# An output projection in halves, full-array masks and sums, and a new order of values and tails in a recurrent attention layer

## Chip, cores, metric

The kernel runs on one core of one Trainium2 chip. The metric is the time of one execution on the device in microseconds (us).

## The reference, cut to what matters

Two kinds of layer alternate, A B A B, over 2048 tokens of 640 features. Layer B is the one that changes. It is a recurrence of 64 steps; each takes 32 tokens and the 8 memory rows that the step before it produced.

```python
for s in range(n_seg):
    h = jnp.concatenate([mem, xs], axis=1)            # 8 + 32 rows
    q, k, v = (einsum('btd,dhe->bhte', h, W) for W in (Wq, Wk, Wv))   # 32 heads of 128
    p = softmax(where(mask, q @ k.T * scale, -1e9))
    o = einsum('bhte,hed->btd', p @ v, Wo)
    mem = o[:, :M, :]                                  # goes into the next step
    outs.append(o[:, M:, :])
```

## The kernel before

All of a step's matrices are thin (32 rows), so nearly all matmuls run as four column tiles of 32 columns side by side. A step does, for its two halves of 16 heads: Q and K (b_Qa, b_Ka, b_Qb, b_Kb), each turned by a 32x32 transpose on DVE; mask and scores into b_SP; exp on ACT; sums over the keys by matmuls with ones; Ln and Exp of the sums on ACT, a product on DVE; V (b_V), the values (b_OTL, four row tiles), their copy to SBUF (b_OTsb), the O projection (b_OPS). The last 8 of each step's 32 tokens go apart, four steps at a time: their Q, K and V for the next four steps ("tails", b_tail) and their O projection for the last four ("deferred O", b_OPSd) serve as filling between. Of every four steps one carries the deferred O, one a layer norm with five full-array transposes (b_lntps).

```python
# O projection: per head four column tiles of 160 columns, 128 matmuls a step
for q in range(4):
    nc.tensor.matmul(self.ps[32*q:32*q+32, :], lhsT=self.src_fn(h), rhs=W.wo[:, h, 160*q:160*q+160],
                     start=(self.p == 0 and e == 0), stop=..., tile_position=(0, 32*q), ...)
...
# order of the second half of a step
vpass(0); scores(1); vpass(1); sums(1); values(0); normalise(1)
take("act", 0, 0); take("act", 0, 1)          # copies of the values to SBUF
fill(1.0)
op.run(4); values(1); take("dve", 1, 0); take("act", 1, 1); op.run(4); op.run(8)
...                                           # transpose of O's memory rows, into the next step's h
fill(9)
```

PSUM has three banks for Q, K, V, scores and tails (b_ps), one for O, two pairs for the values.

## Time and profile before

| | before |
|---|---|
| time | 2634.66 us, median of 3 (2625.54 to 2636.77) |
| TensorE busy | 87% |
| steps of layer B | 126 from start to start, mean 14.76 us: 1860 us |
| instruction packets of 16,384 bytes | 512 |

In the lines of the profile PE is TensorE's matmuls and PEld its weight loads, DVE the vector engine, ACT the scalar engine, POOL GpSimd, SPq the queue that starts transfers; L87 is a line of the kernel (here that of a helper), "<-" leads from what is written to what is read, and "issue" is a wait for nothing that the profile shows. A matmul and its weight load are called a pair.

The prediction below shows the lines of the page, of the waits and of the timeline that carry its argument. One more stretch is from the timeline of TensorE alone: start and length in us, the instruction, output and inputs, shapes, count. A length holds the latency of the last matmul, so what a stage costs is read from its start to the next stage's start.

```profile
426.79 1.28 PE L87 MATMUL b_Kb<-b_wk,b_hT 128*32 128x512 bf16 x20
427.87 0.28 PE L87 MATMUL b_SP<-b_PT,b_blk 128*32 128x160 bf16 x6
...
427.98 1.27 PE L87 MATMUL b_V<-b_wv,b_hT 128*32 128x512 bf16 x19
429.04 0.28 PE L87 MATMUL b_SP<-b_mask,c_identb 128*32 128x160 bf16 x4
429.21 0.37 PE L87 MATMUL b_SP<-b_QT,b_KT 128*32 128x40 bf16 x32
429.43 1.27 PE L87 MATMUL b_V<-b_wv,b_hT 128*32 128x512 bf16 x20
```

Kb takes 1.08 us, sums 0.11, V0 1.06, the second mask 0.17 (0.07 of it work, the rest a wait for K), the scores 0.22: 2.64 us from Kb to V1.

### The profile page before, as it was taken

To read this page: it belongs to the slowest core of one execution; us is meant where nothing else is said; L and a number is where in the kernel's file an instruction comes from. 1 tells how busy PE (TensorE), PEld (TensorE's weight loads), DVE (VectorE), ACT (ScalarE), POOL (GpSimd) and SP (SyncE) were. 2 spreads that over 40 slices of the span, in tenths; PEclk is the share of its full clock that TensorE was granted. 3 is DMA by queue.
4 is the path that set the end of the run, shared out by engine and by line. 5 is a ranking of instruction groups with operands and counts; after the bars stand their busy time and mean duration, and the time that the engine had idled before them with its cause. 6 is when DMAs were issued, how large, how long until landed. Compare 5 with 4: busy or idle time off the path is not lost.

```text
span 2645.6 us, 144539 instructions
## 1 busy us (share of the span) xinstructions
PE 2301.3 (87%) x65166; PEld 1440.4 (54%) x65228; DVE 1600.3 (60%) x3743; ACT 882.3 (33%) x2067; POOL 992.5 (38%) x2333
## 2 busy tenths in 40 slices
PE   6878879999989889888769778799999998989996
PEld 3444446556656556555534444466666665665654
DVE  5666646666656556665556666466666666666654
ACT  5665712222222222222146557122222222222221
POOL 2333434333433334333223334334434333334332
PEclk9888989999999999999978889899999999999999
DMA  6662341111100111100033233400100000101000
GB/s 180 153 162 88 96 132 23 24 22 22 22 22 22 23 23 23 24 19 19 21 97 100 85 101 106 136 19 20 22 20 19 20 20 20 21 19 22 17 17 16
DMA packets 118388, 133.20 MB, mean 50 GB/s; under 512 B 31856, under 2 KB 103552, under 8 KB 115840
## 3 DMA queue, kind: packets, MB, share of 16 engines
q1 hardware_dynamic: 116160, 122.21, 17.6%
q8 instruction: 512, 8.39, 1.4%
q10 hardware_dynamic: 1600, 1.66, 0.2%
q14 instruction: 116, 0.95, 0.1%
HBM read 89.17 MB, written 26.21 MB: 44 GB/s over the span
## 4 chain that ended last, share of the span: by engine, by line
PE 70%; DVE 8%; issue 8%; ACT 3%; POOL 2%; DMA 1%; SPq 0%; DVEq 0%; POOLq 0%; ACTq 0%
PE b_OPS L87 12%; PE b_V L87 11%; PE b_tail L87 8%; PE b_Qa L87 6%; PE b_Ka L87 5%; PE b_Kb L87 5%; PE b_SP L87 4%; PE b_Qb L87 4%; PE b_OTL L87 3%; PE b_OPSd L87 3%; PE a_PP L87 3%; ACT a_PT L87 2%; DVE b_TQ L87 2%; PE a_S L87 2%; DVE a_qk L87 1%
## 5 line engine op out<-in xcount | busy, mean ns | idle before, releaser
L87 PEld LDWEIGHTS <-b_hT 128*32 128x32 bf16 x15520 | 466.3, 96 | 319.4 <-issue 63.7
L87 PE MATMUL b_OPS<-b_wo,b_OTsb 128*32 128x160 bf16 x16384 | 365.8, 234 | 58.9 <-issue 50.9
L87 ACT ACTIVATE b_PT<-b_SP 128x224 bf16<-128x224 f32 x256 | 91.5, 358 | 947.3 <-PE b_SP L87 931.1
L87 PEld LDWEIGHTS <-b_OTsb 128*32 128x32 bf16 x16384 | 289.2, 97 | 120.3 <-issue 68.3
L87 ACT ACTIVATE a_PT<-a_S 128x768 bf16<-128x768 f32 (+1 forms) x384 | 325.5, 891 | 83.5 <-PE a_S L87 76.6
L87 PE MATMUL b_V<-b_wv,b_hT 128*32 128x512 bf16 x5120 | 330.0, 380 | 10.7 <-DVE b_TQ L87 7.9
L87 POOL CAST b_QT<-b_TQ 128x384 bf16<-128x384 f32 x254 | 140.8, 554 | 292.7 <-DVE b_TQ L87 292.5
L87 DVE TENSOR_TENSOR b_PT<-b_PT,b_R 128x160 bf16<-128x160 bf16 (+1 forms) x512 | 215.5, 461 | 45.2 <-ACT b_R L87 44.9
L87 POOL TENSOR_TENSOR b_Rtot<-b_Rtot,b_R 128x160 bf16<-128x160 bf16 x256 | 142.8, 558 | 265.3 <-ACT b_R L87 247.8
L87 DVE STREAM_TRANSPOSE b_TQ<-b_Qa 128x512 f32<-128x512 f32 x128 | 91.8, 717 | 206.8 <-PE b_Qa L87 204.8
L87 POOL CAST b_KT<-b_TQ 128x384 bf16<-128x384 f32 x254 | 142.5, 561 | 181.2 <-DVE b_TQ L87 181.1
L87 DVE CAST b_Vsb<-b_V 128x512 bf16<-128x512 f32 x256 | 175.2, 684 | 34.2 <-PE b_V L87 30.5
L87 ACT CAST b_OTsb<-b_OTL 128x320 bf16<-128x320 f32 x384 | 148.7, 421 | 136.1 <-PE b_OTL L87 136.1
L87 PE MATMUL b_Qa<-b_wq,b_hT 128*32 128x512 bf16 x2560 | 172.5, 381 | 21.0 <-DVE b_hT L87 10.0
L87 POOL TENSOR_SCALAR_AFFINE_SELECT a_PT<-a_PT 128x256 bf16<-128x256 bf16 x256 | 109.2, 431 | 214.1 <-ACT a_PT L87 201.1
L87 PE MATMUL b_Ka<-b_wk,b_hT 128*32 128x512 bf16 x2560 | 170.6, 383 | 0.1
L87 PE MATMUL b_Qb<-b_wq,b_hT 128*32 128x512 bf16 x2560 | 168.1, 380 | 0.0
L87 PE MATMUL b_Kb<-b_wk,b_hT 128*32 128x512 bf16 x2560 | 163.1, 379 | 3.1 <-DVE b_xnbd L87 2.2
L87 PE MATMUL a_PP<-a_xnT,a_wt 128*128 128x512 bf16 x505 | 148.9, 409 | 9.6 <-issue 5.4
L87 DVE STREAM_TRANSPOSE b_TM<-b_OPS 128x160 f32<-128x160 f32 x126 | 43.7, 347 | 187.2 <-PE b_OPS L87 187.0
L87 PE MATMUL a_S<-a_qk 32*128 32x512 bf16 (+3 forms) x1024 | 143.9, 323 | 7.1 <-ACT a_PT L87 5.8
L87 PEld LDWEIGHTS <-b_hx 128*32 128x32 bf16 x3840 | 101.2, 97 | 85.6 <-issue 25.1
(162 smaller groups left out, 3834.7 us busy)
## 6 DMA issues: line engine op xcount, KB each, us to landing
a_wt<-a_wpad SPq DMA_DIRECT2D x112, 160.0 KB
b_wo<-in_B_Wo_dram SPq DMA_DIRECT2D x8, 1280.0 KB
b_XO<-xres SPq DMA_DIRECT2D x512, 15.0 KB
b_Vt<-b_Vtb SPq DMA_DIRECT2D x512, 16.0 KB
a_wvo<-in_A_wo_dram SPq DMA_DIRECT2D x8, 800.0 KB
b_wq<-in_B_Wq_dram SPq DMA_DIRECT2D x20, 256.0 KB
b_wk<-in_B_Wk_dram SPq DMA_DIRECT2D x20, 256.0 KB
xres<-a_xo SPq DMA_DIRECT2D x16, 320.0 KB
```

The source lines that it names most:

```text
L87: r = f(*a, **k)
```

## The change

Its intent is fewer and larger TensorE instructions, and an order that hides the copies and the softmax of the second half.

```diff
 # O in halves: two heads at a time, two column tiles each, 320 columns; the two partial sums are added later
-  for q in range(4):
-      matmul(ps[32*q:32*q+32, :160], lhsT=src(h), rhs=W.wo[:, h, 160*q:160*q+160], tile_position=(0, 32*q))
+  for jj2 in range(2):
+      q = 2 * e + jj2
+      matmul(ps[32*q:32*q+32, :320], lhsT=src(h), rhs=W.wo[:, h, 320*jj2:320*jj2+320], tile_position=(0, 32*q))
...
-  nc.vector.tensor_tensor(out=XO[:], in0=ops[:], in1=XO[:], op=ALU.add)                     # 128 x 160
+  nc.vector.tensor_tensor(out=XO[0:64, :], in0=ops[0:64, :], in1=XO[0:64, :], op=ALU.add)   # 64 x 320, twice
+  nc.vector.tensor_tensor(out=XO[0:64, :], in0=ops[64:128, :], in1=XO[0:64, :], op=ALU.add)
...
 # mask: one full-array matmul; sums: block-diagonal ones, 4 full-array matmuls for 8 tiled ones
-  for j in range(4):
-      matmul(sp[32*j:32*j+32, :, 0:40], lhsT=C.identb[:, 32*j:32*j+32], rhs=mask4, tile_position=(0, 32*j))
+  matmul(sp[:, :, 0:40], lhsT=C.identb[:], rhs=mask4)
...
 # the softmax's reciprocals in the layout of the weights: one product for two
-  tensor_tensor(PT[:, b, :, 16:56] *= R);  tensor_tensor(PT[:, b, :, 0:16] *= R[:, :, 24:40])
+  tensor_tensor(PT[:, b] *= R)
...
 # order
-  vpass(1); sums(1); values(0); normalise(1); take(0, 0); take(0, 1); fill(1.0)
-  op.run(4); values(1); take(1, 0); take(1, 1); op.run(4); op.run(8)
+  V1.run(3); values(0); V1.run(2); sums(1); take(0, 0); take(0, 1); normalise(1)
+  op.run(4); op.run(4); fill(0.44); values(1); fill(0.66)
+  take(1, 0); take(1, 1); flush(); op.run(8)        # flush: turns of finished tails, deferred till here
...
-  late.append(store_deferred)      # residual of the deferred O: after Ka of the next step
+  store_deferred(T - 1, u)         # at once
```

The rows of Wq, Wk, Wv, of the layer norm's output and of the memory are permuted to fit the halves; the layer norm's statistics and its application are taken apart, and in one step of four the residual of O itself is stored at once too.

More of the change, by code (lines that the diff above doesn't have):

```diff
@@ L56, in build_consts, with layernorm_stats @@
     return C
-def layernorm_tile(nc, pool, C, xt, xn_out, name):
+def layernorm_stats(nc, pool, C, xt, name):
     stats = pool.tile([128, 2, nc.vector.BN_STATS_DIM], F32, name=f"{name}_st", tag="ln_st")
@@ L67, in layernorm_tile, with layernorm_apply @@
     nc.gpsimd.tensor_tensor(out=rstd[:], in0=rstd[:], in1=C.mhalf[:, 0:1], op=ALU.pow)
-    nc.vector.tensor_scalar(out=xn_out.rearrange("p (g q d) -> p q g d", q=4, d=32),
-                            in0=xt.rearrange("p (q g d) -> p q g d", q=4, d=32),
+    return mv, rstd
+def layernorm_apply(nc, xt, xn_out, mv, rstd):
+    nc.vector.tensor_scalar(out=xn_out.rearrange("p (g jj d) -> p jj g d", jj=2, d=32),
+                            in0=xt.rearrange("p (jj g d) -> p jj g d", jj=2, d=32),
                             scalar1=mv[:, 0:1], scalar2=rstd[:, 0:1], op0=ALU.subtract, op1=ALU.mult)
@@ L574, in load_B_weights @@
         setattr(W, nm, t)
-        sv = src.rearrange("(q g d) h e -> g q d (h e)", q=4, d=32)
+        sv = src.rearrange("(jj g d) h e -> g jj d (h e)", jj=2, d=32)
         for c in range(NCH):
@@ L578, in load @@
                 for q in range(4):
-                    nc.sync.dma_start(t[32 * q:32 * q + 32, c, :], sv[c, q])
+                    nc.sync.dma_start(t[32 * q:32 * q + 32, c, :], sv[2 * c + q // 2, q % 2])
             loads.append(load)
@@ L606, in pair_tile @@
             return pot.tile([128, 2, 512], F32, name=name, tag="ot")
-        ones = st.tile([128, 128], BF16, name="b_ones")
-        nc.vector.memset(ones[:], 1.0)
+        if general:
+            ones = st.tile([128, 128], BF16, name="b_ones")
+            nc.vector.memset(ones[:], 1.0)
         blk = st.tile([128, 2, 4, 32], BF16, name="b_blk")
@@ L615, in layer_B @@
         if not general:
-            Rtot = st.tile([128, 160], BF16, name="b_Rtot")
+            Rtot = st.tile([128, 4, 40], BF16, name="b_Rtot")
             nc.vector.memset(Rtot[:], 0.0)
-        XO = st.tile([128, 160], F32, name="b_XO")
+        XO = st.tile([64, 320], F32, name="b_XO")
         nc.vector.memset(XO[:], 0.0)
@@ L661, in ln_norm, with ln_apply @@
             xt = ln_x.pop(g)
-            xn = wk.tile([128, D], BF16, name="b_xn", tag="xn")
-            layernorm_tile(nc, sm, C, xt[:], xn[:], "b_ln")
-            ln_n[g] = xn
+            ln_n[g] = xt, layernorm_stats(nc, sm, C, xt[:], "b_ln")
+        def ln_apply(g):
+            xt, (mv, rstd) = ln_n[g]
+            xn = ln_n[g] = wk.tile([128, D], BF16, name="b_xn", tag="xn")
+            layernorm_apply(nc, xt[:], xn[:], mv, rstd)
         def ln_tr(g):
@@ L733, in tail_cols @@
             if T not in hx:
-                hx[T] = wk2.tile([128, NCH, 32], BF16, name="b_hx", tag="hx")
+                hx[T] = wk.tile([128, NCH, 32], BF16, name="b_hx", tag="hx")
                 v = xnT_g[T][:].rearrange("p c (i t) -> p c i t", t=32)[:, :, :, 24:32]
@@ L764, in run, with finish, flush @@
                     if not self.parts:
-                        if self.kind == "V":
-                            evac("act", Vtb[self.T][:, self.b, :], self.ps[:])
-                        else:
-                            d = QTt if self.kind == "Q" else KTt
-                            place("pool", turn(self.ps[:]), self.b, d[self.T], 0, 32, 0)
-                return k
+                        done.append(self.finish)
+                return k
+            def finish(self):
+                if self.kind == "V":
+                    evac("act", Vtb[self.T][:, self.b, :], self.ps[:])
+                else:
+                    d = QTt if self.kind == "Q" else KTt
+                    place("pool", turn(self.ps[:]), self.b, d[self.T], 0, 32, 0)
+        done = []
+        def flush():
+            while done:
+                done.pop(0)()
         def tails_to_seg(s):
@@ L788, in run @@
                 if self.ps is None:
-                    self.ps = self.pool.tile([128, 160], F32, name=self.name, tag=self.tag)
+                    self.ps = self.pool.tile([128, 320], F32, name=self.name, tag=self.tag)
                 while k > 0 and self.p < 16:
@@ L792, in run @@
                         h = self.horder[2 * self.p + e]
-                        for q in range(4):
-                            nc.tensor.matmul(self.ps[32 * q:32 * q + 32, :], lhsT=self.src_fn(h), rhs=W.wo[:, h, 160 * q:160 * q + 160],
-                                             start=(self.p == 0 and e == 0), stop=(self.p == 15 and e == 1),
-                                             tile_position=(0, 32 * q), skip_group_check=True)
+                        for jj2 in range(2):
+                            q = 2 * e + jj2
+                            nc.tensor.matmul(self.ps[32 * q:32 * q + 32, :], lhsT=self.src_fn(h), rhs=W.wo[:, h, 320 * jj2:320 * jj2 + 320],
+                                             start=(self.p == 0), stop=(self.p == 15), tile_position=(0, 32 * q), skip_group_check=True)
                     self.p += 1
@@ L801, in add_out @@
         def add_out(ops, XO, name):
+            nc.vector.tensor_tensor(out=XO[0:64, :], in0=ops[0:64, :], in1=XO[0:64, :], op=ALU.add)
             if out_bf16:
-                xnb = wk.tile([128, 160], BF16, name=name, tag=name)
-                nc.vector.tensor_tensor(out=xnb[:], in0=ops[:], in1=XO[:], op=ALU.add)
+                xnb = wk.tile([64, 320], BF16, name=name, tag=name)
+                nc.vector.tensor_tensor(out=xnb[0:64, :], in0=ops[64:128, :], in1=XO[0:64, :], op=ALU.add)
                 return xnb
-            nc.vector.tensor_tensor(out=XO[:], in0=ops[:], in1=XO[:], op=ALU.add)
+            nc.vector.tensor_tensor(out=XO[0:64, :], in0=ops[64:128, :], in1=XO[0:64, :], op=ALU.add)
             return XO
@@ L818, in layer_B @@
             nc_raw.sync.dma_start(W.wo[:, 8 * q:8 * q + 8, :], wo_src[:, 8 * q:8 * q + 8, :])
-        ln_norm(0); ln_tr(0)
+        ln_norm(0); ln_apply(0); ln_tr(0)
         alloc_h(0)
-        nc.vector.tensor_copy(m0[:, 1, :].rearrange("p (g q d) -> p q g d", q=4, d=32),
-                              m0[:, 0, :].rearrange("p (q g d) -> p q g d", q=4, d=32))
+        nc.vector.tensor_copy(m0[:, 1, :].rearrange("p (g jj d) -> p jj g d", jj=2, d=32),
+                              m0[:, 0, :].rearrange("p (jj g d) -> p jj g d", jj=2, d=32))
         mt = ps_tile([128, NCH, 8], BF16, "b_m0T")
@@ L830, in layer_B @@
                 TailUnit(0, kind, b).run(NCH)
+                flush()
         for Wt, dst in ((W.wq, QT), (W.wk, KT)):
@@ L836, in layer_B @@
         tails_to_seg(0)
-        ln_dma(1); ln_norm(1); ln_tr(1)
+        ln_dma(1); ln_norm(1); ln_apply(1); ln_tr(1)
         deferred = {}
         XOd = {}
-        def deferred_rows(x, T_, q):
-            v = x.rearrange("(t i k) d -> t i k d", i=4, k=32)
-            return v[T_, :, 24:32, 160 * q:160 * q + 160]
         def load_deferred(T_):
-            XOd[T_] = wk.tile([128, 160], F32, name="b_XOd", tag="XOd")
-            for q in range(4):
-                nc.sync.dma_start(XOd[T_][32 * q:32 * q + 32, :], deferred_rows(x_src, T_, q))
+            XOd[T_] = wk.tile([64, 320], F32, name="b_XOd", tag="XOd")
+            for jj2 in range(2):
+                for i in range(4):
+                    r = 32 * (4 * T_ + i) + 24
+                    nc.sync.dma_start(XOd[T_][32 * jj2 + 8 * i:32 * jj2 + 8 * i + 8, :], x_src[r:r + 8, 320 * jj2:320 * jj2 + 320])
         xn_pending = []
@@ L932, in scores @@
                 sp = t[:, 0:224].rearrange("p (r c) -> p r c", c=56)
-                for j in range(4):
-                    nc.tensor.matmul(sp[32 * j:32 * j + 32, :, 0:40], lhsT=C.identb[:, 32 * j:32 * j + 32],
-                                     rhs=mask[:].unsqueeze(1).to_broadcast([128, 4, 40]),
-                                     start=True, stop=False, tile_position=(0, 32 * j), skip_group_check=True)
+                nc.tensor.matmul(sp[:, :, 0:40], lhsT=C.identb[:], rhs=mask[:].unsqueeze(1).to_broadcast([128, 4, 40]),
+                                 start=True, stop=False, skip_group_check=True)
                 for r in range(4):
@@ L955, in sums @@
             def sums(b):
-                sm_ = SP[b][:, 256:416].rearrange("p (r c) -> p r c", c=40)
+                sm_ = SP[b][:, 256:480].rearrange("p (r c) -> p r c", c=56)
                 for k in range(2):
-                    for j in range(4):
-                        o = sm_[32 * j:32 * j + 32, :, 24 * k:40]
-                        nc.tensor.matmul(o, lhsT=blk[:, k, j, :], rhs=PT[:, b, :, 0:16] if k else PT[:, b, :, 16:56],
-                                         start=(k == 0), stop=(k == 1), tile_position=(0, 32 * j), skip_group_check=True)
@@ L964, in normalise @@
-            def normalise(b):
-                R = sm.tile([128, 160], F32, name="b_R", tag="R")
-                nc.scalar.activation(out=R[:], in_=SP[b][:, 256:416], func=ACT.Ln)
-                nc.scalar.activation(out=R[:], in_=R[:], func=ACT.Exp, scale=-1.0)
-                Rv = R[:].rearrange("p (r c) -> p r c", c=40)
-                nc.vector.tensor_tensor(out=PT[:, b, :, 16:56], in0=PT[:, b, :, 16:56], in1=Rv, op=ALU.mult)
-                nc.vector.tensor_tensor(out=PT[:, b, :, 0:16], in0=PT[:, b, :, 0:16], in1=Rv[:, :, 24:40], op=ALU.mult)
+                    lhsT = blk[:, k].rearrange("p j n -> p (j n)")
@@ new lines, in sums @@
+                    first, last_ = (k == 0), (k == 1)
+                    nc.tensor.matmul(sm_[:, :, 40 * k:56] if k else sm_[:, :, 16:56], lhsT=lhsT,
+                                     rhs=PT[:, b, :, 0:16] if k else PT[:, b, :, 16:56],
+                                     start=first, stop=last_, skip_group_check=True)
+                    nc.tensor.matmul(sm_[:, :, 0:16], lhsT=lhsT, rhs=PT[:, b, :, 0:16] if k else PT[:, b, :, 40:56],
+                                     start=False, stop=last_, skip_group_check=True)
@@ L972, in normalise @@
+            def normalise(b):
+                R = wk.tile([128, 4, 56], F32, name="b_R", tag="R")
+                flat = R[:].rearrange("p r c -> p (r c)")
+                nc.scalar.activation(out=flat, in_=SP[b][:, 256:480], func=ACT.Ln)
+                nc.scalar.activation(out=flat, in_=flat, func=ACT.Exp, scale=-1.0)
+                nc.vector.tensor_tensor(out=PT[:, b], in0=PT[:, b], in1=R[:], op=ALU.mult)
                 if not general:
-                    nc.gpsimd.tensor_tensor(out=Rtot[:], in0=Rtot[:], in1=R[:], op=ALU.add)
+                    nc.gpsimd.tensor_tensor(out=Rtot[:], in0=Rtot[:], in1=R[:, :, 16:56], op=ALU.add)
@@ L989, in take, with __init__, run @@
                 evac(eng, OTsb[:, h:h + 8, :].rearrange("p (j r) c -> p j (r c)", j=2), OTL[b, jp][:, :, 0:160])
-            def vpass(b):
-                V = ps_tile([128, 512], F32, "b_V")
-                thin_mm(V, vcols, W.wv, b, w_cols)
-                evac("dve", Vsb[:, b, :], V[:])
+            class VPass:
+                def __init__(self, b):
+                    self.b = b
+                    self.ps = ps_tile([128, 512], F32, "b_V")
+                    self.parts = thin_parts(self.ps, vcols, W.wv, b, w_cols)
+                def run(self, k=NCH):
+                    while k > 0 and self.parts:
+                        self.parts.pop(0)()
+                        k -= 1
+                    if not self.parts:
+                        evac("dve", Vsb[:, self.b, :], self.ps[:])
             qk(W.wq, "b_Qa", 0, QT)
@@ L999, in layer_B @@
                 late.pop(0)()
-            for q in range(4):
-                nc.sync.dma_start(XO[32 * q:32 * q + 24, :], x_src[32 * s:32 * s + 24, 160 * q:160 * q + 160])
+            for jj2 in range(2):
+                nc.sync.dma_start(XO[32 * jj2:32 * jj2 + 24, :], x_src[32 * s:32 * s + 24, 320 * jj2:320 * jj2 + 320])
             qk(W.wq, "b_Qb", 1, QT)
@@ L1014, in layer_B @@
                 row_max(1)
-            vpass(0)
+            VPass(0).run()
             scores(1)
-            vpass(1)
+            V1 = VPass(1)
+            V1.run(3)
+            values(0)
+            g_need = (s + 6) // 4 if s % 4 == 2 else NT
+            if g_need < NT:
+                ln_norm(g_need)
+            V1.run(2)
             sums(1)
-            values(0)
-            normalise(1)
             take("act", 0, 0)
             take("act", 0, 1)
+            normalise(1)
+            if g_need < NT:
+                ln_apply(g_need)
+                xn_pending.append(g_need)
             if i4 != 3:
                 tails_to_seg(s + 1)
-            fill(1.0)
             op = OPass(lambda h: OTsb[:, h, 0:32], HORDER, "b_OPS", po, "op")
             op.run(4)
+            op.run(4)
+            fill(0.44)
             values(1)
+            fill(0.66)
             take("dve", 1, 0)
             take("act", 1, 1)
-            op.run(4)
+            flush()
             op.run(8)
             ops = op.ps
-            g_need = (s + 6) // 4
-            if s % 4 == 2 and g_need < NT:
-                ln_norm(g_need)
-                xn_pending.append(g_need)
             if not general:
@@ L1046, in layer_B @@
             if not last:
-                TM = wk.tile([128, NCH, 32], F32, name="b_TM", tag="TM")
+                TM = wk.tile([128, 10, 32], F32, name="b_TM", tag="TM")
                 nc.vector.transpose(out=TM[:].rearrange("p g t -> p (g t)"), in_=ops[:])
-                nc.vector.tensor_copy(hT[s + 1][:, :, 24:32], TM[:, :, 24:32])
+                for hf in range(2):
+                    nc.vector.tensor_tensor(out=hT[s + 1][64 * hf:64 * hf + 64, :, 24:32], in0=TM[0:64, hf:10:2, 24:32],
+                                            in1=TM[64:128, hf:10:2, 24:32], op=ALU.add)
             fill(9)
+            flush()
             if not last and i4 == 3:
@@ L1056, in store @@
                 xo = add_out(ops, XO, "b_xnb")
-                for q in range(4):
-                    nc.sync.dma_start(x_dst[32 * s:32 * s + 24, 160 * q:160 * q + 160], xo[32 * q:32 * q + 24, :])
-            late.append(store)
+                for jj2 in range(2):
+                    nc.sync.dma_start(x_dst[32 * s:32 * s + 24, 320 * jj2:320 * jj2 + 320], xo[32 * jj2:32 * jj2 + 24, :])
+            if i4 == 1:
+                store()
+            else:
+                late.append(store)
             def store_deferred(T_, od):
@@ L1064, in store_deferred @@
                 xd = add_out(od.ps, XOd.pop(T_), "b_xnbd")
-                for q in range(4):
-                    nc.sync.dma_start(deferred_rows(x_dst, T_, q), xd[32 * q:32 * q + 32, :])
+                for i in range(4):
+                    for jj2 in range(2):
+                        r = 32 * (4 * T_ + i) + 24
+                        nc.sync.dma_start(x_dst[r:r + 8, 320 * jj2:320 * jj2 + 320], xd[32 * jj2 + 8 * i:32 * jj2 + 8 * i + 8, :])
             for u in units:
                 if isinstance(u, OPass):
-                    late.append(lambda u=u, T=T: store_deferred(T - 1, u))
+                    store_deferred(T - 1, u)
             if last:
@@ L1078, in layer_B @@
             rt = sm.tile([128, 1], F32, name="b_rt", tag="seen")
-            nc.vector.tensor_reduce(out=rt[:], in_=Rtot[:], axis=AX.X, op=ALU.add)
+            nc.vector.tensor_reduce(out=rt[:], in_=Rtot[:].rearrange("p r c -> p (r c)"), axis=AX.X, op=ALU.add)
             nc.vector.tensor_tensor(out=C.tot[:, 1, 0:1], in0=C.tot[:, 1, 0:1], in1=rt[:], op=ALU.add)
```

## The prediction

> **What bounds the kernel now.** The chip ran 2634.66 us (median of 3). I read the page first: which engine is busy, the chain that ended last, and the costliest groups.
>
> ```profile
> PE 2301.3 (87%) x65166; PEld 1440.4 (54%) x65228; DVE 1600.3 (60%) x3743; ACT 882.3 (33%) x2067; POOL 992.5 (38%) x2333
> ...
> q8 instruction: 512, 8.39, 1.4%
> ...
> PE 70%; DVE 8%; issue 8%; ACT 3%; POOL 2%; DMA 1%; SPq 0%; DVEq 0%; POOLq 0%; ACTq 0%
> ...
> L87 PE MATMUL b_OPS<-b_wo,b_OTsb 128*32 128x160 bf16 x16384 | 365.8, 234 | 58.9 <-issue 50.9
> ```
>
> TensorE is the chain (70%), with 8% "issue", where it waited for nothing that the profile shows. The second line is a hint at what that is: a queue that moves instructions brought 512 packets, 8.39 MB, so 16,384 bytes each; at 64 bytes that is 256 instructions, and 512 x 256 is about the 130,394 matmuls and weight loads of the first line. I then looked at who TensorE waited for over the whole run (columns: who, for whom, us in total, times, longest):
>
> ```profile
> PE b_OPS L87 <- issue: 50.9, 68, 1.5
> ...
> PE b_OPSd L87 <- issue: 26.6, 22, 1.7
> ...
> PE b_OTL L87 <- issue: 18.3, 24, 1.6
> PE b_tail L87 <- issue: 12.1, 16, 1.6
> ```
>
> The unexplained waits sit in the O projection (b_OPS, b_OPSd), in the values (b_OTL) and just behind them: where instructions are smallest. The timeline of TensorE alone there (start, length, instruction, count):
>
> ```profile
> 848.28 0.25 PE L87 MATMUL b_OPS<-b_wo,b_OTsb 128*32 128x160 bf16 x2 [0.92 <-issue]
> 848.46 0.20 PE L87 MATMUL b_OTL<-b_PT,b_Vsb 32*128 32x40 bf16 x4
> ...
> 848.65 0.17 PE L87 MATMUL b_OTL<-b_PT,b_Vt 8*128 8x16 bf16 x4
> 848.76 2.00 PE L87 MATMUL b_OPS<-b_wo,b_OTsb 128*32 128x160 bf16 x94
> 851.75 0.25 PE L87 MATMUL b_OPS<-b_wo,b_OTsb 128*32 128x160 bf16 x2 [1.00 <-issue]
> ```
>
> From stall to stall there are 2+32+94 = 128 matmuls, with their loads 256 instructions: one packet. They took 851.75-848.28 = 3.47 us although the work ended about 1 us sooner. At 910.40 and 914.42 another such pair has 67+61 = 128 matmuls between, 4.02 us. So one block of 256 instructions costs at least about 3.5 us (27 ns per load-and-matmul pair), sometimes 4, however short its work is. Each stall is the shortfall of one block.
>
> Layer B runs twice with 64 steps each. From the first b_Qa of a step to the next I get a mean of 14.76 us over 126 steps (10th percentile 13.8, least 13.4): 15.7 for steps that carry the deferred O projection (one in four), 14.3 to 14.6 for the others. So 1860 of the 2645 us are these steps, and a step without stalls costs about 13.5.
>
> **What the Trainium skill says.** "Runtime: NRT & Kernel Launch", section "Instruction fetch mechanics": instructions are refilled in 16 KiB blocks of 256, and the fetch is mostly hidden. The block size agrees with the 16,384-byte packets; "hidden" does not, as above. "TensorE: Matmul & The Clock Gate", "Back-to-back issue gap": N/2.4 + 2.5 ns per warm matmul, 216 ns at N=512. A clean b_Ka of 20 matmuls (five rounds of four column tiles) takes 1.08 us from its start to b_Qb's, 216 ns a round: agrees. "TensorEngine Tiling (Array Packing)", "Key Properties": a change of tiling mode drains the array. The trace shows its size where the row-tiled values meet column-tiled work:
>
> ```profile
> 417.78 0.19 PE L87 MATMUL b_OTL<-b_PT,b_Vsb 32*128 32x40 bf16 x4
> 417.81 0.18 PE L87 MATMUL b_OTL<-b_PT,b_Vt 8*128 8x16 bf16 x4
> 417.91 1.26 PE L87 MATMUL b_tail<-b_wk,b_hx 128*32 128x512 bf16 x20
> ```
>
> Groups of values follow each other after 0.02 to 0.03 us, the switch takes 0.10: about 0.09 us a switch. "VectorE: DVE Perf Modes", the TRN2 errata section: an fp32 two-tensor add takes (N+151)/0.96 ns; b_XO at N=160 measures 325 ns against 324.
>
> **The change, part by part.** All per step, 126 steps counted.
>
> O in halves. 32 heads x 4 matmuls of 160 columns become 32 x 2 of 320. Streaming is unchanged: 32 rounds of 160 or 16 of 320. Before, 96 of them in a clean stretch take 1.81 us (419.98 to 421.79), 18.9 ns each, and 32 take 0.66. After, I scale by the formula: 320/2.4+2.5 = 136 ns a round of four, 34 ns each, 64 in 2.17 us against 2.47: -0.3. The deferred pass gains likewise. The larger gain is the fetch: pairs of 34 ns are slower than the 27 ns the fetch sustains.
>
> Instruction count. O: -64 matmuls; deferred O -64 in one step of four; masks -6; sums -8. That is -78 (-94 on average with the deferred part), each with a load: from 924 instructions (3.6 blocks, 12.6 us at 3.5) to 736 (2.9 blocks, 10.1 us). The tightest window of 128 pairs afterwards, by the new order: scores(1) 32 pairs 0.22 us, 12 of V1 0.74, values(0) 0.39, 8 of V1 0.43, sums 0.24, 32 of O 1.08, 8 of fill 0.43: 3.5 us, just the floor. So nearly all fetch stalls go; I leave 0.1 for blocks that take 4 us. This removes the gap 14.76-13.65 = about 1.1 us (13.65 is the clean mean by kind of step: three at 13.5 to 13.7 and one with the transposes of a layer norm at 13.9).
>
> Switches. Mask and sums become full-array matmuls and the values cut V1 in two. Before 4 switches, after 12: +8 x 0.09 = 0.7 us. Not all count: at mask(0) TensorE waits some 0.3 us for DVE's K transposes anyway (mask to scores 0.36 us in clean steps, 0.17 at scores(1)), so those two are hidden, and at scores(1) about 0.1 goes the same way, because the slower sums give DVE time. Left: about 0.5 us. The sums stream 160+64+64+64 = 352 columns where four tiles side by side took the time of 224: +0.05 us each by 2.4 columns per ns, +0.1 together.
>
> Softmax on ACT and DVE. R widens from 160 to 224 elements: +0.05 us on each ACT pass (305 and 337 ns now; the 224-wide exp takes 358). Two DVE products (440+483 ns) become one, which I put at 0.5. R(0) is ready 0.15 later through sums and ACT, the product ends 0.35 earlier.
>
> DVE elsewhere. Two adds of 320 (491 ns each by the formula) for one of 325: +0.66, into DVE's 0.58 us idle before the Kb transpose: nearly hidden. The transpose for the memory goes from 347 ns to about 515 (from the 717 of 512 columns), and two adds (0.2 each) replace one cast of 0.18: chain from O to the next Qa 0.6 -> 1.05 us, beside 1.08 us of fill: +0.1 at most.
>
> Waits. values(0) moves ahead by 8 pairs of V1 and sums: V0's cast ends about 2.6 us after Kb, TensorE gets there at 2.5: +0.1. values(1): Ln now follows two takes on ACT; takes end about 0.95 us after values(0), Ln and Exp 0.75, product 0.5, so 2.35; TensorE brings V1 0.52, sums 0.24, O 1.08, fill 0.43 = 2.3: even.
>
> Sum: 13.65 - 0.3 (O) + 0.5 (switches) + 0.1 (sums) - 0.1 (scores(1)) + 0.05 (ACT) + 0.2 (memory chain and values(0)) = 14.1; less the wait for the first copies before O that is now hidden (0.1), and with 0.1 of fetch stalls left still 14.1; I take 14.0, since most of these small waits can overlap. 14.76-14.0 = 0.76 x 126 = 96 us: 2634.66 - 96 = 2538.
>
> **Rivals.** (a) Switches take the place of the fetch: if all eight cost 0.1 to 0.14 us unhidden, a step is 14.4 and the time 2590. For it: the layer-norm transposes put 0.1 us on each side of them. Against: half of the switches lie in waits for DVE. (b) DVE becomes the bound at the softmax: it is 60% busy, its adds grow and its chain through R is longer; 0.3 us more per step gives 2575. Against: in a step of 13.8 us (735.30 to 749.10) it is busy 7.94 us, and the fused product gives back what the adds take. (c) The switches overlap better than I think and the fetch stalls hidden under 380 ns matmuls also go: a step of 13.5, 2475. (d) The fetch stalls were only an effect of the profiler: then little changes but O's 0.3 less 0.5, and the time stays near 2640. Against: the profiled run is only 0.4% longer than the timed ones.
>
> **Range and chances.** The count of instructions is certain, the floor of 3.5 to 4 us well seen; unsure are the cost of switches and the new waits, each about 0.3 us per step either way (38 us). That gives 2475 to 2595. Faster by over 2% means under 2582: (a) in full, (d) or (b) with (a) must come true to miss it. I give 0.85, 0.13 within 2%, 0.02 slower.
>
> **What would show it.** TensorE's waits for "issue" at b_OPS, b_OPSd, b_OTL should fall from over 100 us to under 30; instruction packets from 512 to about 415; b_OPS 8192 matmuls, b_OPSd 2048; rounds of O at 136 ns; switches of 0.09 us at mask and sums; a step of 14.0. Wrong: issue waits that stay, O slower than 34 ns per matmul, TensorE waiting for DVE b_PT or b_Vsb by over 0.3 us a step, or masks that cost over 0.3 us at scores(1).

## The result

The changed kernel takes 2557.3 us (median of 4, 2554.6 to 2560.73), the kernel before 2632.14 in the same rounds. The ratio is 0.9718 (0.9693 to 0.9744): faster by 2.8%. A later repeat gave 2564.11 us and 0.972.

The lines of the page after, which answer to those of before:

```profile
PE 2346.4 (92%) x53196; PEld 1266.5 (50%) x53196; DVE 1668.9 (65%) x3771; ACT 921.6 (36%) x2067; POOL 1014.8 (40%) x2333
...
q8 instruction: 418, 6.85, 1.1%
...
L91 PE MATMUL b_OPS<-b_wo,b_OTsb 128*32 128x320 bf16 x8192 | 325.3, 300 | 5.4 <-DVE b_OTsb L91 5.3
```

There are 53,196 matmuls for 65,166, 418 instruction packets for 512. TensorE's busy share rises, because what stood idle went. The idle time before b_OPS fell from 58.9 to 5.4 us, and "issue" is no longer named there. The waits of TensorE alone over the whole run (who, for whom, us, times, longest) now begin with layer A's; those of layer B are small:

```profile
PE b_Qa L91 <- DVE b_hT L91: 19.1, 66, 1.2
...
PE b_V L91 <- DVE b_TQ L91: 8.1, 28, 0.3
...
PE b_OPS L91 <- DVE b_OTsb L91: 5.3, 8, 0.7
```

The stretch from Kb to V1, as shown of before:

```profile
652.66 1.28 PE L91 MATMUL b_Kb<-b_wk,b_hT 128*32 128x512 bf16 x20
653.87 0.33 PE L91 MATMUL b_SP<-b_PT,b_blk 128*128 128x160 bf16 x4
654.13 1.26 PE L91 MATMUL b_V<-b_wv,b_hT 128*32 128x512 bf16 x20
655.33 0.24 PE L91 MATMUL b_SP<-b_mask,c_identb 128*128 128x160 bf16 x1
655.50 0.37 PE L91 MATMUL b_SP<-b_QT,b_KT 128*32 128x40 bf16 x32
655.72 0.84 PE L91 MATMUL b_V<-b_wv,b_hT 128*32 128x512 bf16 x12
```

Shapes 128*128 are the full-array matmuls. The same stretch is 3.06 us where it was 2.64: Kb 1.21, sums 0.26, V0 1.20. Fewer instructions, and 0.42 us longer.

I summed, over the steps of both layers B, each stage's time from its start to the next stage's (a wait counts to the stage before it):

| us in 126 steps | before | after |
|---|---|---|
| b_OPS | 387.2 | 286.5 |
| b_OPSd | 98.1 | 77.5 |
| b_OTL (values) | 102.1 | 78.4 |
| b_SP (mask, scores, sums) | 200.5 | 180.8 |
| b_Qa and b_Ka | 288.0 | 274.5 |
| b_Qb and b_Kb | 275.9 | 309.3 |
| b_V | 276.2 | 317.7 |
| b_tail | 221.5 | 240.8 |
| b_lntps | 10.7 | 7.7 |
| sum | 1860.1 | 1773.2 |

Where instructions are many and small, 145 us went (the first three rows); b_Qb, b_Kb, b_V and b_tail took 94 back (15 of them, at b_Qb, is a switch that run 3 shows to be free: b_SP has the less to wait). The mean step fell from 14.76 to 14.07 us.

### The profile page after: what moved, and what is told of

It is laid out like the page before. It is cut to its first block, busy times and chain, and to the rows that moved or that the text cites. A ratio compares the mean times of both kernels' runs of the same rounds, so it can differ in the third digit from the quotient of the medians.

```text
span 2552.9 us, 119988 instructions
## 1 busy us (share of the span) xinstructions
PE 2346.4 (92%) x53196; PEld 1266.5 (50%) x53196; DVE 1668.9 (65%) x3771; ACT 921.6 (36%) x2067; POOL 1014.8 (40%) x2333
## 5 line engine op out<-in xcount | busy, mean ns | idle before, releaser
L91 PEld LDWEIGHTS <-b_hT 128*32 128x32 bf16 x15520 | 418.9, 96 | 332.0 <-issue 46.0
L91 PE MATMUL b_V<-b_wv,b_hT 128*32 128x512 bf16 x5120 | 348.4, 382 | 8.1 <-DVE b_TQ L91 8.1
L91 PE MATMUL b_OPS<-b_wo,b_OTsb 128*32 128x320 bf16 x8192 | 325.3, 300 | 5.4 <-DVE b_OTsb L91 5.3
L91 POOL TENSOR_TENSOR b_Rtot<-b_Rtot,b_R 128x160 bf16<-128x160 bf16 x256 | 158.2, 618 | 306.0 <-ACT b_R L91 306.0
L91 PEld LDWEIGHTS <-b_OTsb 128*32 128x32 bf16 x8192 | 195.9, 96 | 100.6 <-DVE b_OTsb L91 50.2
L91 PE MATMUL b_Qa<-b_wq,b_hT 128*32 128x512 bf16 x2560 | 162.9, 382 | 22.1 <-DVE b_hT L91 19.1
L91 DVE TENSOR_TENSOR b_PT<-b_PT,b_R 128x224 bf16<-128x224 bf16 x256 | 118.6, 463 | 79.0 <-ACT b_R L91 76.3
L91 PE MATMUL a_PP<-a_xnT,a_wt 128*128 128x512 bf16 x560 | 155.2, 413 | 2.3 <-DVE a_t1k L91 0.9
L91 DVE STREAM_TRANSPOSE b_TM<-b_OPS 128x320 f32<-128x320 f32 x126 | 65.1, 517 | 115.2 <-PE b_OPS L91 115.2
L91 DVE CAST a_qk<-a_PP 128x512 bf16<-128x512 f32 x128 | 88.0, 688 | 70.0 <-PE a_PP L91 70.0
```

Of the source, the lines that this page charges most:

```text
L91: r = f(*a, **k)
```

## The experiments

The theory: the O projection in halves removes waits for the fetch of instructions, and the switches between column-tiled and full-array matmuls give part back. The rival: the new order, the fused product and the deferred turns made it faster, and the number of instructions does not matter. Twelve kernels ran; all were correct. Two first builds of the second kernel did not fit in SBUF; moving b_R and b_hx to single buffers, as the change does, made room. One caution on ratios: the kernel before took 2639, 2656 and 2637 us, the last two on the same chip. So kernels of different calls are compared by their own times and by the mean step in their traces, where the changed kernel has 2557 to 2564 us and 14.07 to 14.10.

### 1. The old number of instructions in the new kernel

```diff
-  matmul(ps[q rows, 0:320], lhsT=src(h), rhs=wo[:, h, 320 columns], ...)
+  for hf in range(2):      # the same work, the same column tile, in two of 160
+      matmul(ps[q rows, 160*hf:160*hf+160], lhsT=src(h), rhs=wo[:, h, 160 columns], ...)
```

> The changed kernel, but each matmul of the O projection of 320 columns is issued as two of 160 with the same weights, to the same column tile: same streaming, same order, same switches, 80 more load-and-matmul pairs a step (896 instructions in place of 736). Theory (the gain is the fetch of instructions): the waits for 'issue' at b_OPS, b_OPSd and b_OTL come back, 0.5 to 1.0 us a step, so the time goes from 2557 to 2620 to 2690 us. Rival (the gain comes from the new order, the fused product and the deferred turns, and the number of instructions does not matter): within 15 us of 2557.

Measured: 2666.39 us, ratio 1.0097. That is 102 to 109 us over the changed kernel (2564.11 and 2557.3), and 1% slower than the kernel before. TensorE's waits:

```profile
PE b_OPSd L91 <- issue: 28.2, 30, 1.4
...
PE b_OPS L91 <- issue: 23.0, 33, 1.6
...
PE b_OTL L91 <- issue: 13.5, 25, 1.1
```

The waits for "issue" are back at the three places where they were before, and nothing but the count of instructions differs from the changed kernel. The rival falls. The mean step is 14.92 us. The streaming costs the same: a round of four column tiles takes 69 ns at 160 columns and 136 at 320 (medians). In the steps there are 107 waits for "issue" here (157 before, none in the changed kernel); read from one matmul's start to the next one's, they take 98 us, nearly the whole difference.

The trace also holds the packets that bring instructions, and they tie "issue" to the fetch. All 157 of these waits in the steps of before, and all 107 here, ended 1.2 to 1.6 us after such a packet had landed (median 1.4). For 126 random moments in the steps of before the same distance runs from -1.3 (a packet still under way) to 5.8 us. The packets never began closer than 3.1 us to each other.

### 2. O in halves alone

> The kernel before with the O projection in halves alone (and what it needs: rows of weights, residual and memory in halves): masks, sums, order and turns as before. 80 pairs a step fewer, no new switches of tiling mode. Theory: it has all of the gain or more, 2490 to 2560 us, with a step of 13.6 to 14.0. Rival (the order, the fused product and the deferred turns gave it): 2600 to 2640.

The edit is the kernel before with the O part of the diff above and what belongs to it (permuted rows, two additions, memory), everything else as before. Measured: 2568.0 us, ratio 0.9727. So the halves alone bring nearly the whole gain, but not more: 8 us beyond the range that I expected, with a mean step of 14.16 us where I had at most 14.0. The trace tells why: in steps that follow a deferred O, Kb starts 1.65 us late (1.50 of it is idle time, the rest is latency of the matmul before). From the timeline (all engines; the bracket is the idle time before and who ended it):

```profile
667.79 1.01 DVE L87 TENSOR_TENSOR b_XOd<-b_OPSd,b_XOd 64x320 f32<-64x320 f32 x2
...
668.86 1.26 PE L87 MATMUL b_Kb<-b_wk,b_hT 128*32 128x512 bf16 x20 [1.50 <-DVE b_XOd L87]
```

Kb needs the bank that holds the deferred O until its residual is added, and the two larger additions of XO and XOd stand in one queue after Ka. The change moves this addition ahead; run 9 adds that one line.

### 3. The mask in four tiles again

```diff
-  matmul(sp[:, :, 0:40], lhsT=C.identb[:], rhs=mask4)
+  for j in range(4):
+      matmul(sp[32*j:32*j+32, :, 0:40], lhsT=C.identb[:, 32*j:32*j+32], rhs=mask4, tile_position=(0, 32*j))
```

> The changed kernel with the mask in four column tiles again: 6 pairs more and 4 switches of tiling mode fewer in a step. Theory (a switch costs about 0.1 us where nothing hides it): nothing at scores(0), which waits for DVE, and 0.15 to 0.2 us at scores(1), so 18 to 25 us off, 2532 to 2540. Rival (the switch is hidden, or the one-matmul mask saves its own cost): 2555 to 2570.

Measured: 2540.12 us, ratio 0.962; mean step 13.94.

```profile
655.26 1.26 PE L91 MATMUL b_V<-b_wv,b_hT 128*32 128x512 bf16 x20
656.35 0.24 PE L91 MATMUL b_SP<-b_mask,c_identb 128*32 128x160 bf16 x4
656.42 0.39 PE L91 MATMUL b_SP<-b_QT,b_KT 128*32 128x40 bf16 x32
```

V0 takes 1.09 us to the mask where it took 1.20, the mask 0.07 where it took 0.17: a switch costs 0.10 to 0.11 us, on each side of the one-matmul mask. At scores(0) both kernels start the scores 3.58 us into the step, because DVE's turn of K sets that time: there the switches are free, as predicted. Three matmuls saved, 0.21 us paid. The mean step falls by 0.14 us only, so later waits take part of it back; which, I did not follow.

### 4. The sums in four tiles again

```diff
+  for j in range(4):
-  matmul(sm_[:, :, cols], lhsT=blk[:, k] as 128x128, rhs=PT...)
+      matmul(sm_[32*j:32*j+32, :, cols], lhsT=blk[:, k, j, :], rhs=PT..., tile_position=(0, 32*j))
```

> The changed kernel with the sums in four column tiles again (224 columns wide as now, so the fused product stays): 12 pairs more and 4 switches fewer in a step. Theory: Kb to sums 0.14 and sums to V 0.1 us shorter, and as much around sums(1), 0.3 to 0.45 us a step, less up to 0.15 us of new fetch stalls: 20 to 50 us off, 2505 to 2540. Rival (the switches overlap other waits): 2550 to 2570.

Measured: 2543.48 us, ratio 0.9634; mean step 13.95. The gain is there, but 3 us short of the range that I expected: Kb goes back from 1.22 to 1.08 us, but sums(0) to V0 stays at 0.29 in about half of the steps, and the waits for "issue" show again (4.8 us in the steps). My expectation miscounted the edit, and so does that of run 11: a step's two sums are 32 matmuls in place of 8, so 24 pairs more and not 12 (the trace has 442 instruction packets for 418).

### 5. V1 in one piece

```diff
-  V1.run(3); values(0); V1.run(2); sums(1)
+  V1.run(5); sums(1); values(0)
```

> The changed kernel with V1 in one piece again: V1, sums(1), values(0), then the copies and O. Two switches of tiling mode fewer in a step. Theory (the split hides the copies of values(0), some 0.6 us of ACT before O can start): O waits 0.3 to 0.5 us a step for b_OTsb, less 0.1 to 0.2 for the switches, so 2570 to 2610 us. Rival (the split only costs switches): 2530 to 2545.

Measured: 2639.67 us, ratio 0.9945: 75 to 82 us slower than the changed kernel, more than I expected. One line of TensorE's waits tells it: 128 waits, one in each step, of 0.63 us on average.

```profile
PE b_OPS L91 <- ACT b_OTsb L91: 80.7, 128, 0.9
```

O now follows the values at once, and stands for ACT's copy of them. The split pays for its two switches many times over, in this order.

### 6. Turns of the tails not deferred

```diff
-  done.append(self.finish)     # run later by flush()
+  self.finish()
```

> The changed kernel with the turns of the tails made as soon as their last part is issued, so before the copies of values(1) on DVE and ACT, not after them. Theory (a turn of 0.72 us on DVE, or a copy of 0.59 on ACT, before a copy that O waits for): 0.2 to 0.5 us in three steps of four, 2575 to 2605 us, with TensorE's waits for b_OTsb up. Rival (O has enough else before it): 2550 to 2565.

Measured: 2652.35 us, ratio 0.9987: 88 to 95 us slower than the changed kernel, far more than I expected. From the timeline (all engines) of a step with Q tails:

```profile
705.33 0.72 DVE L91 STREAM_TRANSPOSE b_TQ<-b_tail 128x512 f32<-128x512 f32 x1 [0.92 <-PE b_tail L91]
705.97 0.45 DVE L91 CAST b_OTsb<-b_OTL 128x320 bf16<-128x320 f32 x1
...
706.47 1.27 PE L91 MATMUL b_OPS<-b_wo,b_OTsb 128*32 128x320 bf16 x32 [1.20 <-DVE b_OTsb L91]
```

My expectation counted the 0.72 us of the turn. But the kernel fixes the order of DVE's instructions, so the copy of the values behind the turn also waits until the tail's last matmul is done: DVE sat idle 0.92 us, most of it with the values ready (ACT began its copy of their other half at 704.63). Together TensorE stands 1.20 us before O. The new order puts a tail's last parts just before this copy, and only the deferral makes that harmless.

### 7. The layer norm's transposes in another bank

```diff
-  tps = ps_tile([128, NCH, 128], BF16, "b_lntps")            # one of the three banks
+  tps = pot.tile([128, NCH, 128], BF16, name="b_lntps", tag="ot")   # the values' pool, free then
```

> The changed kernel with the transposes of the layer norm in a bank of the values' pool, which is free then, not in one of the three banks that Qb, Kb, V0 share. Theory (in every fourth step the transposes take the bank that V0 needs, and V0 waits for the turn of Kb; that step lasts 14.7 us against 13.85): 0.3 to 0.5 us off that step, 9 to 16 us in all, 2541 to 2549. Rival (the step is longer for the switches and the transposes themselves): within 4 us of 2557.

Measured: 2547.82 us, ratio 0.9596 (beside the slow 2656). First the changed kernel, TensorE alone, then this one:

```profile
695.87 0.32 PE L91 MATMUL b_SP<-b_PT,b_blk 128*128 128x160 bf16 x4
696.48 1.26 PE L91 MATMUL b_V<-b_wv,b_hT 128*32 128x512 bf16 x20 [0.29 <-DVE b_TQ L91]
```

```profile
696.00 0.32 PE L91 MATMUL b_SP<-b_PT,b_blk 128*128 128x160 bf16 x4
696.25 1.26 PE L91 MATMUL b_V<-b_wv,b_hT 128*32 128x512 bf16 x20
```

From sums to V0 it is 0.61 us in the changed kernel and 0.25 here. The mean of the steps with a layer norm falls from 14.67 to 14.26 us: 0.41 in 30 steps, 12 us.

### 8. Runs 3, 4 and 7 together

> The changed kernel with mask and sums in column tiles and the layer norm's transposes in the values' pool. If the three gains add (17 + 14 + 12 us): 2514. If the transposes and casts of Kb on DVE take the place of the switches before scores(1): 2522 to 2535.

Measured: 2529.91 us; mean step 13.87. The gains do not add. TensorE now reaches values(0) before DVE has copied V0; by my sum over the steps it stands 18 us for b_Vsb there and 12 us for b_KT at the scores. This was the second of the two expectations.

### 9. O in halves alone, with the deferred residual stored at once

```diff
 # on run 2
-  late.append(lambda: store_deferred(T - 1, u))
+  store_deferred(T - 1, u)
```

> O in halves alone (as in the second run), but with the residual of the deferred O added and stored at once at the end of its step, as the changed kernel has it, not after Ka of the next. In the second run Kb of every fourth step began 1.65 us late, waiting for that addition, which frees its bank. Theory: this wait goes, 1.3 to 1.65 us in 32 steps, so 41 to 53 us off the second run: a ratio to before of 0.952 to 0.958. Rival (the additions only move in front of the turn of Qa, and the wait comes back there): 0.968 to 0.973, as the second run.

Measured: 2526.34 us, ratio 0.9576 (0.9558 to 0.9594). The late Kb is gone, and the steps after a deferred O fall from 14.82 to 13.45 us. This kernel has neither the full-array mask and sums, nor the split V1, nor the deferred turns, and it is faster than the whole change, which took 2564.11 (0.972). The sum of stages, made for this run too, tells what the rest of the change does: b_OPS takes 321.8 us here against 286.5, so the new order does hide 35 us at O; but b_V (272.9 against 317.7) and b_Kb (143.7 against 157.3) are 58 us shorter here.

### 10. and 11. A version that beats both

```diff
 # on run 8; run 11 has this and the tiled mask, but full-array sums
-  evac("dve", Vsb[:, self.b, :], self.ps[:])
+  evac("act" if self.b == 0 else "dve", Vsb[:, self.b, :], self.ps[:])
```

> The eighth run's kernel, with V0 copied out of PSUM by ACT in place of DVE. There values(0) waited 18 us in all for b_Vsb of DVE, whose queue has the turn and cast of Kb and the product before it. Theory: this wait goes, and DVE loses 0.69 us a step: 12 to 20 us off, a ratio to before of 0.945 to 0.948 (the eighth run has 0.9525). Rival (the product of DVE is then the last to come, or ACT's copy delays the exponential of scores(1)): 0.951 to 0.954.

Measured for run 10: 2508.04 us, ratio 0.9504 (0.9483 to 0.9525), mean step 13.67. The time fell by 22 us from run 8, and TensorE's waits for b_Vsb, 18 us there, are gone, as the theory says. The ratio lies between the theory's figures and the rival's; both were set from a call in which before took 2656 us, not 2637. Runs 8 and 10 are of these two calls, so a part of the 22 us may be the call's; the wait that went is in the traces. This is the fastest kernel.

> As the tenth run, but with the sums as full-array matmuls, as in the changed kernel: 12 pairs fewer and 4 switches more in a step. Tells whether column-tiled sums pay once DVE is not before values(0). Theory (they do, as in the fourth run): 0.2 to 0.6 per cent slower than the tenth run. Rival (their instructions cost fetch stalls that eat the gain): equal or faster than the tenth run.

Measured for run 11: 2519.33 us, ratio 0.9554, 0.5% slower than run 10: tiled sums pay.

### 12. The changed kernel again

> The changed kernel again, unchanged, beside the others and beside before on this chip: the kernel before took 2632, 2639 and 2656 us in three calls. Theory (before waits for instructions and this kernel hardly does, so before varies from chip to chip and this one little): 2550 to 2565 us, whatever before takes here. Rival (the chips differ as a whole): a ratio to before of 0.970 to 0.974 again.

Measured: 2564.11 us, ratio 0.972. Both expectations hold, so it separates nothing: before happened to take 2637 us here. That before took 2656 and 2637 us on one chip shows that it is not the chip alone; what it is stays open.

## Why the prediction was right, and where its sums were off

The time on record was 2538 with 2475 to 2595; 2557.3 lies within, and "faster by over 2%" came true. Step by step:

**The bound and the fetch: shown.** Waits for "issue" in the steps were predicted to fall from over 100 to under 30 us; they fell from 124 to nothing (waits of over 0.15 us). Packets: about 415 predicted, 418. Run 1 puts O's instructions back without anything else, and 102 to 109 us and the waits come back with them. That each wait ends 1.2 to 1.6 us after a packet of instructions has landed ties it to the fetch. The 0.1 us a step that I left for remaining stalls was not needed.

**O: right.** Predicted 34 ns a matmul, 2.17 us a step. Rounds of four begin 136 ns apart (median of 2244), as predicted. In the sum over the steps, 8064 matmuls take 286.5 us: 36 ns, with the switches and small waits at the ends.

**Switches: nearly right in size, too generous in what hides them.** 0.09 us each was predicted; 0.10 to 0.11 were measured at the mask, and 0.14 where Kb meets the sums (1.22 for 1.08 us). That the two at scores(0) are free is shown by run 3. The failed term is "- 0.1 (scores(1))": I let DVE's time hide part of the second mask's switches, but they came in full, 0.21 us, because the longer sums had already given DVE all the time it needed: in the stretch shown its copy of K ended at 655.12, before the mask began at 655.33.

**Values(0), values(1): right, or better.** A wait of 0.1 us a step and an even race were predicted; TensorE's waits for b_Vsb and b_PT are under 1 us in all steps together. Runs 5 and 6 show how closely this order is balanced.

**The memory chain: mis-sized.** The term was "+0.1 at most". From the timeline (all engines) of the changed kernel:

```profile
687.89 1.27 PE L91 MATMUL b_OPS<-b_wo,b_OTsb 128*32 128x320 bf16 x32
...
688.99 1.25 PE L91 MATMUL b_tail<-b_wq,b_hx 128*32 128x512 bf16 x20
689.21 0.52 DVE L91 STREAM_TRANSPOSE b_TM<-b_OPS 128x320 f32<-128x320 f32 x1 [0.44 <-PE b_OPS L91]
689.76 0.53 DVE L91 TENSOR_TENSOR b_hT<-b_TM 64x40 bf16<-64x40 f32 x2
...
690.44 0.83 PE L91 MATMUL b_Qa<-b_wq,b_hT 128*32 128x512 bf16 x12 [0.20 <-DVE b_hT L91]
```

The durations were as predicted (0.52 for the transpose, 0.43 to 0.53 for the two additions), but I had left out most of the way between engines: 0.22 us from where the next stage follows O to the transpose (0.17 of it latency of O's last matmul, whose modelled end is at 689.16) and 0.15 from the sum to Qa. In this step the filling of 1.08 us covers a chain of 1.45; in most clean steps of the trace the last fill starts at 12.48 of 13.83 us, so about 0.27 us are uncovered.

**The layer-norm step: a term missed.** I set the clean step of 13.9 us, of before, under the same sum, which makes 14.3; it takes 14.67. The transposes hold a bank, and V0 waits for the turn of Kb; the two longer additions stand ahead of it in DVE's queue. Run 7 shows the bank's part: 0.41 us. That the additions are what made it worse than before is argued from DVE's order, not tested.

**The sum.** Step: 14.0 predicted, 14.07 measured; these errors cancel in part, so that it came this close is partly luck. The base of 13.65 was shaky too: it takes three kinds of step as 13.5 to 13.7 when clean, but of the steps with the deferred O the quickest in the trace lasted 13.83 and the next 14.59. The rest of the 19 us lies in how I applied the difference. I took a step from a profiled execution of before that lasted 2647.3 us and subtracted the difference from a timed median of 2634.66. Between the two profiled spans the difference is 2645.6 - 2552.9 = 93 us, close to my 96; between the timed medians it is 75.

**What I did not see.** I treated the change as one thing with one sum. Runs 9 and 12, side by side, take it apart: O in halves and the early deferred store give 110 us, and the rest of the change costs 38 of them (2564.11 - 2526.34). My own list had the terms (0.5 us for switches, 0.1 for sums, which is 76 us in 126 steps), but I did not ask whether the parts that cause them were needed once O's instructions were halved. Nor did I see that the early store was needed: without it, run 2 shows Kb waiting 1.5 us. What the new order is worth stays open: run 10, the fastest, has it, but whether ACT's copy of V0 would help run 9 as much no run shows.

## What to carry to other kernels

If an engine waits for nothing that the profile names, count its instructions between the stalls against the size of the instruction packets; where they match, as here, larger instructions pay and smaller ones with the same work do not. Fewer instructions are not cheaper by themselves: a full-array matmul between column-tiled ones paid 0.1 us of switch on each side to save three matmuls of a tile. Take a change apart on the chip, for one part can carry more than the whole; and before a copy is put behind another instruction in an engine's queue, ask what that other one waits for, not only how long it runs.

## What the Trainium skill lacked or had wrong

- "Runtime: NRT & Kernel Launch", section "Instruction fetch mechanics", calls the fetch mostly hidden. Its block of 256 instructions agrees with the trace (512 packets of 16,384 bytes), but packets never began closer than 3.1 us here and nine in ten were 3.5 us or more apart (27 ns a pair of load and matmul), and TensorE stood waiting: 80 pairs a step more, with the same work, cost 102 to 109 us (run 1).
- "TensorEngine Tiling (Array Packing)", section "Key Properties", says that a change of mode drains the array, without a size: 0.10 to 0.14 us a switch here (runs 3 and 4), free where TensorE waits anyway (scores(0)).
- "TensorE: Matmul & The Clock Gate", section "Back-to-back issue gap", gives its formula for an isolated matmul and says that it over-counts in a stream of loads and matmuls (131 ns at 512 columns). On column tiles it held in such a stream: 216 ns a round of 512 columns, 136 ns a round of 320.
- No page that I read gives the time from one engine's end to the start of the engine that waits for it as it shows in a trace; here 0.05 us from TensorE's modelled end to DVE and 0.15 from DVE to TensorE, and leaving this and the last matmul's latency out was among the largest slips in a term.
